# P.V of each two-head unit as one block of matmuls in a windowed attention ahead of two FFNs

## The chip, the cores and the metric

One core of one Trainium2 chip. The metric is device microseconds of one launch, the median of three runs. The kernel has four stages on the same core, one after the other: attention, the first FFN, the second FFN, and the stores. Engines are named as the profile names them: PE is TensorE (its matmuls), PEld its weight loads, DVE is VectorE, ACT is ScalarE, POOL is GpSimd, SP issues most DMAs. L270 is line 270 of the kernel before.

## The reference

`q`, `k`, `v` are (4, 8, 576, 64) in float32: 4 batches, 8 heads, 576 positions, head size 64.

```python
scores = scale * np.matmul(q, k.transpose(0, 1, 3, 2))
bias = slopes[:, None, None] * (-np.abs(rel).astype(np.float32))[None, :, :]
mask = (rel >= 0) & (rel < window)          # window = 128
scores = np.where(mask, scores + bias[None], -1000000000.0)
attn = np.exp(scores - np.max(scores, axis=-1, keepdims=True))
attn = attn / (np.sum(attn, axis=-1, keepdims=True) + 1e-09)
x = np.matmul(attn, v)                      # then laid out as (2304, 512)
h = x @ w_in;  g = h * (1.0 / (1.0 + np.exp(-1.702 * h)));  x = g @ w_out
h = x @ w_in;  g = np.where(h >= 1, h, np.where(h <= -1, 0, (h + 1) ** 2 / 4));  x = g @ w_out
```

Each FFN is 512 to 2048 to 512; its weights arrive as 64-bit floats.

## The kernel before, in words

Attention is cut into 16 **units**, one batch and one pair of heads each. A unit has five **steps**, m = 0 to 4, of 128 queries (the last of 64). For a step, two groups of 64 queries of both heads are multiplied with the 192 keys that the window lets them see. The work of a unit is:

- `load_qk`, `load_v`: the DMAs (L162 to L180).
- `trans_qk` (L192): q and k are transposed on PE in three pieces, copied out of PSUM by DVE and ACT (L195, L198). The third piece has only 64 rows.
- `scores` (L209): the score matmuls of a step into one of three `ps_s` banks; DVE adds the bias and takes the maximum (L217) into one of five `p` buffers, ACT takes the exponential (L220).
- `norm`: DVE makes the reciprocal of the sum (L227, L228), POOL multiplies the probabilities with it (L231).
- `trans_p`: PE transposes the probabilities of a step into one of two `ps_t` banks (L246, L247; L253, L254 in the last step), ACT copies them to the tile `pt` (L249 to L256).
- `pv_mm` (L258 to L281): P.V. The matmuls of one portion read key block m - 1 of `v` as weights, 64 columns for each head, and 256 columns of `pt` (128 in the last portion). The heads write partitions 0 to 63 and 64 to 127 of one PSUM bank, `ps_x`. The last portion adds the 64 positions beyond 512 in a second bank `x1`, taken from the pool `ps_a` (L278, L280), and ACT and DVE copy the result to `xt` (L275, L281).

The order in which these functions are called is set by keys: step s = 5u + m calls `scores` at s, `norm` at s + 0.74, `trans_p` at s + 3.5 and, before the change, `pv_mm` at s + 8.05, so a unit's four portions come at four places between the scores and transposes of the next two units. On top of that a scheduler orders each engine's instructions anew; what it made of the keys is seen only in the built order. Every engine then executes its own list in that order.

Meanwhile the weights of the first FFN come in: 32 halves of 512 KB, each converted by five DVE instructions (L59 to L66), one of ACT (L68) and one of POOL (L69). About 15 are converted during attention and the others during the first block of FFN 1. `split_block` (L95, L96) prepares the first block's input from `xt`. FFN 1 runs five blocks of tokens, FFN 2 six; each is a row of matmuls L330 and L381 or L383.

A matmul on float32 is two instructions in the trace: the 128 program matmuls of L270 are 256 there.

Of the kernel before, what the change touches and what calls it, by code (L numbers as in the profile page):

```python
# [10 lines left out]
F32 = mybir.dt.float32  # L11
# [10 lines left out]
P = 128  # L22
# [3 lines left out]
def tile_window_attention_two_ffn(ctx: ExitStack, tc: tile.TileContext, q, k, v, w1_in, w1_out, w2_in, w2_out, out):  # L26
    nc = tc.nc
# [69 lines left out]
            parts.append(xs)  # L97
        return parts

# [1 line left out]
    with ExitStack() as actx:  # L101
        def pool(name, bufs, **kw):
            return actx.enter_context(tc.tile_pool(name=name, bufs=bufs, **kw))
# [7 lines left out]
        ps_a = pool("ps_a", 2, space=PSUM)  # L111
        ps_s = pool("ps_s", 3, space=PSUM)
        ps_t = pool("ps_t", 2, space=PSUM)
        ps_x = pool("ps_x", 1, space=PSUM)
# [36 lines left out]
        NM = 5  # L151
# [103 lines left out]
                nc.scalar.copy(pt[:, n - 2, :], ps[:, 0, :])  # L255
                nc.scalar.copy(pt[0:64, n - 1, :], ps[0:64, 1, :])  # L256

        def pv_mm(u, m):  # L258
            b, hp = units[u]
            d = st[u]  # L260
            pt, vr = d["pt"], d["v"]
            kb = m - 1
            t0 = b * S
            heads = [slice(64 * j, 64 * j + 64) for j in range(2)]
            if m == 1:
                d["x"] = ps_x.tile([P, 512], F32, tag="x", name="ps_x")
            x = d["x"]
            n = 4 if m < NM - 1 else 2
            for r in heads:
                nc.tensor.matmul(  # L270
                    x[r, 128 * kb:128 * kb + 64 * n].rearrange("p (a b) -> p a b", b=64), vr[:, kb, r],
                    pt[:, 4 * kb:4 * kb + n, r], start=(kb == 0), stop=(m == NM - 1), skip_group_check=True)
            if m < NM - 1:
                return
            nc.scalar.copy(xt[hp][:, t0:t0 + 512], x)  # L275
            x1 = ps_a.tile([P, 2, 256], F32, tag="a", name="ps_x1")
            for r in heads:
                nc.tensor.matmul(x1[r, 0, 0:64], vr[:, kb, r], pt[:, 4 * kb + 2, r], start=True, stop=False)  # L278
            for r in heads:
                nc.tensor.matmul(x1[r, 0, 0:64], vr[0:64, m, r], pt[0:64, 4 * kb + 3, r], start=False, stop=True)  # L280
            nc.vector.tensor_copy(xt[hp][:, t0 + 512:t0 + S], x1[:, 0, 0:64])  # L281

        ev = []
# [1 line left out]
        def at(key, fn, *args):  # L285
            ev.append((key, len(ev), fn, args))
# [4 lines left out]
        for u in range(NU):  # L291
            if u > 0:
                at(5 * u - 2.87, load_qk, u)
                at(5 * u - 13.98, load_v, u)
            for c in range(3):
                at(5 * u - 1.58 + c * 1.49 if u > 0 else -99 + c, trans_qk, u, c)
            for m in range(NM):
                s = 5 * u + m
                at(s, scores, u, m)
                at(s + 0.74, norm, u, m)  # L300
                at(s + 3.5, trans_p, u, m)
                if m > 0:
                    at(s + 8.05, pv_mm, u, m)
        for f in range(SPLIT):
            for i in range(2):
                at(19.59 + 9.45 * (f + 0.5 * i), load_w1, f, i)
# [1 line left out]
            fn(*args)  # L308
        xs0 = split_block(0, B1[0])

# [1 line left out]
    w_b = ctx.enter_context(tc.tile_pool(name="w_b", bufs=NF - SPLIT, reuse_waits="tile"))  # L312
    g_p = ctx.enter_context(tc.tile_pool(name="g_p", bufs=2, reuse_waits="tile"))
    ps_o = ctx.enter_context(tc.tile_pool(name="ps_o", bufs=5, space=PSUM, reuse_waits="tile"))
# [148 lines left out]
```

## Time and profile before

| what | us |
|---|---|
| median of 3 runs (lowest, highest) | 996.01 (995.71, 996.92) |
| span of the profiled execution, first to last instruction | 995.0 |
| median less that span | 1.0 |
| PE busy, share of the span | 967.3, 97% |
| DVE busy | 581.0, 58% |
| ACT busy | 382.9, 38% |
| POOL busy | 160.8, 16% |

The page gives no time of the profiled execution but its span. The span has two unlike parts. Up to about 162 us it is attention, with PE, DVE and ACT all busy most of the time; after that it is the FFNs, in which PE is busy nearly always, and DVE beside it only while weights are converted (to about 248 us, and again at about 500 to 650 us). The busy shares of the whole span hide this, so the views by stage and the chain of work are what to read.

### The profile page before, as it was taken

The numbers are of one execution on the slowest core, as the hardware profiler recorded it, in microseconds if no ns is written. First come the engines' busy times: TensorE is split into PE (matmuls) and PEld (weight loads), VectorE is DVE, ScalarE is ACT, GpSimd is POOL, SyncE is SP. The second block draws the span as 40 slices with busy tenths as digits, with TensorE's granted clock in tenths as the row PEclk, the third lists the DMA queues.
The fourth block names the chain that finished last, engine by engine and source line by source line (L and its number), as shares of the span: only waits on it lengthen the run. The fifth ranks groups of instructions, "written<-read, shape, count | busy, mean of one in ns | idle before, by whom it ended". The sixth has DMA issues, their size and how long they took to land.

```text
span 995.0 us, 13850 instructions
## 1 busy us (share of the span) xinstructions
PE 967.3 (97%) x5024; PEld 837.6 (84%) x5024; DVE 581.0 (58%) x1403; ACT 382.9 (38%) x928; POOL 160.8 (16%) x232
## 2 busy tenths in 40 slices
PE   7999999997999999999999899999999999999998
PEld 5767777876889999999888789789999999999997
DVE  5788889999422422422379999953444444434443
ACT  5898886323222322322333333342332322423322
POOL 4565564232000000000023223300000000000000
PEclk9999999999999999999999999999999999999999
DMA  5565543333000000000013323200000000000000
GB/s 135 150 150 149 147 130 106 119 127 127 1 1 1 1 0 1 1 1 1 1 45 127 126 85 121 91 32 1 1 32 1 13 20 1 33 1 1 32 1 33
DMA packets 81972, 53.33 MB, mean 54 GB/s; under 512 B 58992, under 2 KB 75632, under 8 KB 81904
## 3 DMA queue, kind: packets, MB, share of 16 engines
q1 hardware_dynamic: 81760, 52.31, 18.0%
q8 instruction: 40, 0.66, 0.3%
q14 instruction: 28, 0.23, 0.1%
q10 hardware_dynamic: 144, 0.13, 0.0%
HBM read 47.71 MB, written 4.72 MB: 53 GB/s over the span
## 4 chain that ended last, share of the span: by engine, by line
PE 84%; DVE 11%; issue 2%; SPq 1%; ACT 1%; DMA 0%; POOL 0%; DVEq 0%; POOLq 0%
PE ph L330 35%; PE o L383 17%; PE o L381 17%; PE ps_s L209 4%; PE ps_x L270 4%; DVE x L62 2%; PE ps_qk L192 2%; DVE x L64 2%; PE ps_t L246 2%; DVE x L60 1%; PE ps_t L247 1%; DVE x L66 1%; DVE gs L343 1%; DVE x L59 1%; DVE xs L96 1%
## 5 line engine op out<-in xcount | busy, mean ns | idle before, releaser
L330 PE MATMUL ph<-xs,w 128*128 128x384 f32 (+2 forms) x2112 | 434.1, 354 | 3.4 <-ACT xs L95 1.9
L330 PEld LDWEIGHTS ph<-xs,w 128*128 128x128 f32 x2112 | 386.6, 189 | 34.3 <-DVE xs L96 2.7
L381 PE MATMUL o<-gs,w 128*128 128x460 f32 (+1 forms) x960 | 216.2, 374 | 10.2 <-ACT gs L342 9.2
L383 PE MATMUL o<-w,gs 128*128 128x512 f32 x864 | 216.8, 395 | 2.4 <-ACT gs L342 2.3
L381 PEld LDWEIGHTS o<-gs,w 128*128 128x128 f32 x960 | 180.4, 189 | 34.4 <-ACT gs L342 12.7
L383 PEld LDWEIGHTS o<-w,gs 128*128 128x128 f32 x864 | 160.8, 188 | 34.3 <-ACT gs L342 3.8
L342 ACT CAST gs<-ph 128x384 fp32r<-128x384 f32 (+2 forms) x176 | 89.5, 508 | 188.0 <-DVE ph L341 115.9
L69 POOL TENSOR_TENSOR w<-x,w 128x512 fp32r<-128x512 f32 x64 | 86.2, 1348 | 422.8 <-ACT w L68 419.4
L343 DVE TENSOR_TENSOR gs<-ph,gs 128x384 fp32r<-128x384 f32 (+2 forms) x176 | 104.3, 592 | 77.7 <-ACT gs L342 77.5
L340 DVE TENSOR_TENSOR ph<-ph,ga 128x384 f32<-128x384 f32 x96 | 54.2, 564 | 142.7 <-ACT ga L339 142.7
L337 DVE TENSOR_TENSOR ph<-ph,ga 128x460 f32<-128x460 f32 (+1 forms) x80 | 51.4, 642 | 142.2 <-ACT ga L336 142.2
L339 ACT ACTIVATE ga<-ph,half 128x384 f32<-128x384 f32 x96 | 55.8, 581 | 140.7 <-PE ph L330 135.4
L336 ACT ACTIVATE ga<-ph 128x460 f32<-128x460 f32 (+1 forms) x80 | 44.3, 554 | 152.6 <-PE ph L330 152.4
L231 POOL TENSOR_SCALAR p<-p,sm 128x192 f32<-128x192 f32 (+1 forms) x144 | 69.9, 497 | 64.7 <-DVE sm L228 25.7
L68 ACT CAST w<-x 128x512 fp32r<-128x512 f32 x64 | 39.6, 621 | 85.5 <-DVE x L66 84.2
L220 ACT ACTIVATE p<-p,sm 128x192 f32<-128x192 f32 (+1 forms) x144 | 62.0, 433 | 11.1 <-DVE sm L217 9.8
L209 PE MATMUL ps_s<-kt,q 128*128 128x192 f32 (+2 forms) x288 | 60.1, 329 | 0.0
L341 DVE SCALAR_TENSOR_TENSOR ph<-ga,ph 128x384 f32<-128x384 f32 x96 | 53.8, 560 | 2.8
L217 DVE CUSTOM_DVE_ANT_0 p<-ps_s,bias 128x192 f32<-128x192 f32 (+1 forms) x144 | 45.2, 329 | 15.8 <-PE ps_s L209 12.6
L62 DVE TENSOR_SCALAR x<-x 128x512 int32<-128x512 int32 x64 | 49.6, 776 | 1.2
L209 PEld LDWEIGHTS ps_s<-kt,q 128*128 128x128 f32 x288 | 44.7, 196 | 6.1 <-ACT pt L251 1.5
L64 DVE SCALAR_TENSOR_TENSOR x<-raw,x 128x512 int32<-128x512 int32 x64 | 45.9, 719 | 1.3
(57 smaller groups left out, 601.0 us busy)
## 6 DMA issues: line engine op xcount, KB each, us to landing
raw<-in_moe_w_in_dram SPq DMA_DIRECT2D x32, 512.0 KB, 3.7
raw<-in_moe_w_out_dram SPq DMA_DIRECT2D x32, 512.0 KB, 3.5
out_dram<-ob SPq DMA_DIRECT2D x17, 256.0 KB, 2.0
vraw<-in_v_dram SPq DMA_DIRECT2D x32, 128.0 KB, 2.6
qkraw<-in_q_dram SPq DMA_DIRECT2D x30, 128.0 KB, 2.7
qkraw<-in_k_dram SPq DMA_DIRECT2D x30, 128.0 KB, 2.6
qkraw<-in_q_dram SPq DMA_DIRECT2D x16, 32.0 KB, 2.4
qkraw<-in_k_dram SPq DMA_DIRECT2D x16, 32.0 KB, 2.4
```

The source lines that it names most:

```text
L62: nc.vector.tensor_scalar(out=x, in0=x, scalar1=3, scalar2=0x3FFFFFF8, op0=ALU.logical_shift_left, op1=ALU.bitwise_and)
L64: nc.vector.scalar_tensor_tensor(out=x, in0=lo, scalar=29, in1=x, op0=ALU.logical_shift_right, op1=ALU.bitwise_or)
L69: nc.gpsimd.tensor_tensor(out=w[:, 1, i, :], in0=f32(x), in1=f32(w[:, 0, i, :]), op=ALU.subtract)
L209: nc.tensor.matmul(ps[:, e, lo:192], d["q"][:, i, :], d["k"][:, 64 * i - 128 + lo:64 * i + 64], start=True, stop=True)
L220: nc.scalar.activation(x, x, AF.Exp, bias=sm[:, 0, e:e + 1], scale=-1.0, accum_out=sm[:, 1, e:e + 1])
L231: nc.gpsimd.tensor_scalar(out=x, in0=x, scalar1=sm[:, 2, e:e + 1], scalar2=1.0, op0=ALU.mult, op1=ALU.mult)
L330: nc.tensor.matmul(ph, w[f][:, a, 0, c * P:(c + 1) * P], xs[j][c][:, b, :], start=(c == 0 and i == 0), stop=(c == KC - 1 and i == 2))
L339: nc.scalar.activation(a, ph, AF.Relu, scale=0.5, bias=half)
L342: nc.scalar.copy(gs[:, 0, :], ph)
L343: act_last[0] = nc.vector.tensor_tensor(out=gs[:, 1, :], in0=ph, in1=f32(gs[:, 0, :]), op=ALU.subtract)
L381: nc.tensor.matmul(o[j][m][:, 0:n], w[f][:, a, 1, sl], gs[:, b, :], start=first, stop=last)
L383: nc.tensor.matmul(o[j][m], gs[:, b, sl], w[f][:, a, 1, :], start=first, stop=last)
```

## The change

`pv_mm(u, m)`, called four times for a unit, becomes `pv_unit(u)`, called once at the key of the former last portion. It issues the same matmuls on the same operands, those of the bank `x` first and then those of `x1`, and then the two copies. The key of every other function is as before.

```diff
-        def pv_mm(u, m):
+        def pv_unit(u):
...
-            kb = m - 1
...
-            if m == 1:
-                d["x"] = ps_x.tile([P, 512], F32, tag="x", name="ps_x")
-            x = d["x"]
-            n = 4 if m < NM - 1 else 2
+            x = ps_x.tile([P, 512], F32, tag="x", name="ps_x")
+            x1 = ps_a.tile([P, 2, 256], F32, tag="a", name="ps_x1")
+            last = NM - 1
+            for kb in range(last):
+                n = 4 if kb < last - 1 else 2
+                for r in heads:
+                    nc.tensor.matmul(
+                        x[r, 128 * kb:128 * kb + 64 * n].rearrange("p (a b) -> p a b", b=64), vr[:, kb, r],
+                        pt[:, 4 * kb:4 * kb + n, r], start=(kb == 0), stop=(kb == last - 1), skip_group_check=True)
             for r in heads:
-                nc.tensor.matmul(
-                    x[r, 128 * kb:128 * kb + 64 * n].rearrange("p (a b) -> p a b", b=64), vr[:, kb, r],
-                    pt[:, 4 * kb:4 * kb + n, r], start=(kb == 0), stop=(m == NM - 1), skip_group_check=True)
-            if m < NM - 1:
-                return
+                nc.tensor.matmul(x1[r, 0, 0:64], vr[:, last - 1, r], pt[:, 4 * last - 2, r], start=True, stop=False)
+            for r in heads:
+                nc.tensor.matmul(x1[r, 0, 0:64], vr[0:64, last, r], pt[0:64, 4 * last - 1, r], start=False, stop=True)
             nc.scalar.copy(xt[hp][:, t0:t0 + 512], x)
...
-                if m > 0:
-                    at(s + 8.05, pv_mm, u, m)
+            at(5 * u + 4 + 8.05, pv_unit, u)
```

The scheduler makes its own order of this, so a unit's matmuls are not one uninterrupted run on PE. In the built order L274 and L276 are the former L278 and L280, and the line numbers from there on are lower by 4. A **cluster** below is a run of P.V matmuls with nothing else of PE between them. In the order before there are 66 clusters; in the order of the change there are 39.

PE around the second step of a unit, before (`p_107` and `p_108` are the probability buffers of steps 1 and 2, `q_112` the queries of the next unit; the second pair of transposes of a step is left out):

```order
L270 MATMUL ps_x<-pt,vraw 64x256 x2
L246 MATMUL ps_t<-ident,p_107 128x128
L247 MATMUL ps_t<-ident,p_107 128x128
...
L192 MATMUL ps_qk<-ident,qkraw 128x128 x4
L270 MATMUL ps_x<-pt,vraw 64x256
L209 MATMUL ps_s<-kt,q_112 128x64
L209 MATMUL ps_s<-kt,q_112 128x128
L270 MATMUL ps_x<-pt,vraw 64x256
L246 MATMUL ps_t<-ident,p_108 128x128
```

The same place in the changed order:

```order
L192 MATMUL ps_qk<-ident,qkraw 128x128
L246 MATMUL ps_t<-ident,p_107 128x128
L247 MATMUL ps_t<-ident,p_107 128x128
...
L192 MATMUL ps_qk<-ident,qkraw 128x128 x3
L270 MATMUL ps_x<-pt,vraw 64x256 x3
L209 MATMUL ps_s<-kt,q_112 128x64
L209 MATMUL ps_s<-kt,q_112 128x128
L246 MATMUL ps_t<-ident,p_108 128x128
```

Three clusters of two, one and one matmuls have become one of three, ahead of the next unit's first scores.

PE further on in the same unit, before (steps 3 and 4):

```order
L209 MATMUL ps_s<-kt,q_112 128x192 x2
L270 MATMUL ps_x<-pt,vraw 64x256 x2
L192 MATMUL ps_qk<-ident,qkraw 128x64 x2
L246 MATMUL ps_t<-ident,p_109 128x128
...
L209 MATMUL ps_s<-kt,q_112 128x192 x2
L270 MATMUL ps_x<-pt,vraw 64x128 x2
L278 MATMUL ps_x_605<-pt,vraw 64x64 x2
L280 MATMUL ps_x_605<-pt,vraw 64x64 x2
L253 MATMUL ps_t<-ident,p_110 128x128
```

The same place in the changed order:

```order
L209 MATMUL ps_s<-kt,q_112 128x192 x2
L192 MATMUL ps_qk<-ident,qkraw 128x64 x2
L246 MATMUL ps_t<-ident,p_109 128x128
...
L209 MATMUL ps_s<-kt,q_112 128x192 x2
L270 MATMUL ps_x<-pt,vraw 64x256 x3
L270 MATMUL ps_x<-pt,vraw 64x128 x2
L274 MATMUL ps_x_596<-pt,vraw 64x64 x2
L276 MATMUL ps_x_596<-pt,vraw 64x64 x2
L253 MATMUL ps_t<-ident,p_110 128x128
```

The cluster ahead of the 64-row transposes L192 is gone, and its matmuls stand in the unit's last cluster.

POOL around step 3, the same in the two orders at this place (`p_108` and `p_109` belong to steps 2 and 3):

```order
L231 TENSOR_SCALAR p_108<-p_108,sm 128x192 x2
L69 TENSOR_TENSOR w<-x,w 128x512
L231 TENSOR_SCALAR p_109<-p_109,sm 128x192 x2
```

A weight's instruction L69 stands directly ahead of the two normalisations of step 3 in 4 units of the order before and in 5 of the changed one.

## Rows read from the trace of the kernel before

**Rows 1.** Busy time by stage: stretch, its length, each engine (instructions), PE clock.

```profile
core 0: us, PE busy (x) PEld busy (x) DVE busy (x) ACT busy (x) POOL busy (x), PEclk, DMA share, GB/s
20.00:162.00 142.00, 141.10 (x1030) 101.71 (x1029) 119.81 (x588) 126.30 (x436) 84.25 (x149) 1.00 0.56 142
162.00:210.00 48.00, 46.93 (x223) 41.50 (x222) 46.71 (x74) 16.67 (x30) 14.48 (x11) 1.00 0.36 116
210.00:250.00 40.00, 32.37 (x143) 26.52 (x142) 37.90 (x61) 13.14 (x25) 9.15 (x7) 0.98 0.38 124
```

**Rows 2.** The chain that ended last, 60 to 66 us: start, length, engine, tile, line.

```profile
60.03 0.58 PE ps_x L270 x4
60.62 0.26 PE ps_t L246
60.88 0.11 PE ps_t L247
60.99 0.11 PE ps_t L246
...
61.64 0.57 PE ps_x L270 x2
62.22 0.64 PE ps_s L209 x4
62.86 0.58 PE ps_x L270 x2
63.44 0.26 PE ps_t L246
...
64.68 0.58 PE ps_x L270 x4
65.26 0.27 PE ps_qk L192 x2
65.53 0.26 PE ps_t L246
```

**Rows 3.** The same chain at two longer clusters.

```profile
99.30 1.01 PE ps_x L270 x6
...
152.85 1.66 PE ps_x L270 x14
```

**Rows 4.** Groups by line, 0 to 225 us: P.V matmuls and their weight loads.

```profile
L270 PE MATMUL ps_x<-pt,vraw 128*64 128x256 f32 (+1 forms) x256 | 45.3, 374 | 0.0
L270 PEld LDWEIGHTS ps_x<-pt,vraw 128*64 128x64 f32 x256 | 16.8, 135 | 15.0 <-issue 11.4 <-ACT pt L256 0.9
```

**Rows 5.** The same chain where the 64-row transposes follow scores, not P.V.

```profile
148.39 0.65 PE ps_s L209 x4
149.05 0.27 PE ps_qk L192 x2
149.31 0.26 PE ps_t L246
```

**Rows 6.** The same chain where the weights' conversion carries it, in FFN 1's first block.

```profile
226.32 1.50 DVE x L62
227.84 0.70 DVE x L64
228.57 0.70 DVE x L66
229.29 0.62 ACT w L68
229.91 0.49 ACT gs L342
```

**Rows 7.** Timeline of PE: step 3's scores in two units, its transposes in the first.

```profile
58.24 0.33 PE L209 MATMUL ps_s<-kt,q 128*128 128x192 f32 x1
...
65.46 0.33 PE L246 MATMUL ps_t<-ident,p 128*128 128x128 f32 x1
...
77.20 0.49 PE L209 MATMUL ps_s<-kt,q 128*128 128x192 f32 x2
```

**Rows 8.** Timeline of POOL in the second of these units.

```profile
81.72 1.27 POOL L69 TENSOR_TENSOR w<-x,w 128x512 fp32r<-128x512 f32 x1
82.97 0.59 POOL L231 TENSOR_SCALAR p<-p,sm 128x192 f32<-128x192 f32 x1
```

More of the change, by code (lines that the diff above doesn't have):

```diff
@@ L261, in pv_mm @@
             pt, vr = d["pt"], d["v"]
-            kb = m - 1
             t0 = b * S
             heads = [slice(64 * j, 64 * j + 64) for j in range(2)]
-            if m == 1:
-                d["x"] = ps_x.tile([P, 512], F32, tag="x", name="ps_x")
-            x = d["x"]
-            n = 4 if m < NM - 1 else 2
-            for r in heads:
-                nc.tensor.matmul(
-                    x[r, 128 * kb:128 * kb + 64 * n].rearrange("p (a b) -> p a b", b=64), vr[:, kb, r],
-                    pt[:, 4 * kb:4 * kb + n, r], start=(kb == 0), stop=(m == NM - 1), skip_group_check=True)
-            if m < NM - 1:
-                return
-            nc.scalar.copy(xt[hp][:, t0:t0 + 512], x)
[L276 to L280, printed above, removed]
+            x = ps_x.tile([P, 512], F32, tag="x", name="ps_x")
[7 more added lines that the diff above has]
+                        pt[:, 4 * kb:4 * kb + n, r], start=(kb == 0), stop=(kb == last - 1), skip_group_check=True)
+            for r in heads:
+                nc.tensor.matmul(x1[r, 0, 0:64], vr[:, last - 1, r], pt[:, 4 * last - 2, r], start=True, stop=False)
+            for r in heads:
+                nc.tensor.matmul(x1[r, 0, 0:64], vr[0:64, last, r], pt[0:64, 4 * last - 1, r], start=False, stop=True)
+            nc.scalar.copy(xt[hp][:, t0:t0 + 512], x)
             nc.vector.tensor_copy(xt[hp][:, t0 + 512:t0 + S], x1[:, 0, 0:64])
```

## The prediction

> **What bounds the kernel now.** I began with the busy time by stage [rows 1], since shares of the whole span mix two kernels. From 20 to 162 us, nearly all of attention, PE is busy for 141.1 of 142 us, but ACT is busy for 126.3 (89%) and DVE for 119.8 (84%), so that view alone doesn't settle which of them sets the pace. The chain of work does: from 60 to 66 us [rows 2] every piece is a PE instruction released by the PE instruction before it, and so it goes on through the attention stage. What shortens PE's own list there should shorten the stage, as long as the other engines keep up.
>
> The reader should see three things in those rows. A cluster of one pair of matmuls, one for each head (x4 in the trace), lasts 0.58 us. A cluster with a single matmul (x2) lasts 0.57 us, just as long: the two heads run beside each other, and a lone one leaves its partner's place empty. And the first transpose behind a cluster takes 0.26 us where the following ones take 0.11, so each cluster also makes its follower 0.15 us longer.
>
> From 162 us the limit is another. DVE is busy for 46.7 of 48 us and then 37.9 of 40 [rows 1], and late in this stretch the chain goes through the conversion of weights [rows 6]. That work is fixed and waits for nothing of the change. In both orders 15 of the 32 halves are converted ahead of the last unit's copy on DVE, so the rest begins earlier by what attention ends earlier, and the gain should arrive at the end undiminished.
>
> **What the change removes.** The matmuls themselves stay. What goes is the cost of starting and ending a cluster. Its price comes from longer clusters [rows 3]: x6 is two pair slots and takes 1.01 us, so a further slot costs 1.01 - 0.58 = 0.43 us. The long one confirms it: three full slots and one of half width are 0.58 + 0.43 + 0.43 + 0.22 = 1.66. A one-slot cluster costs 0.58 + 0.15 = 0.73 us, of which 0.43 is work; **0.30 us is the price of having a cluster**. The weight loads tell of the same thing: they sat idle for 15.0 us ahead of L270, 11.4 of it with no releaser ("issue") [rows 4], which is 0.23 us for each of 66 clusters.
>
> Would merging also fill empty places? No: counted by slots of 256 columns, a lone matmul counting as a full slot, the order before needs 63 and the changed one 63 too, since the scheduler again cuts runs at odd places. So only the fixed price counts: 66 - 39 = 27 clusters by 0.30 us are 8.1 us.
>
> One correction. Ten of the removed clusters stood directly ahead of the 64-row transposes L192. There the followers are 0.27 and 0.26 us [rows 2], and where the same transposes follow scores they are 0.27 and 0.26 as well [rows 5]. The delay behind the cluster belongs to those transposes and stays. These ten save 0.58 - 0.43 = 0.15 us each instead of 0.30, which takes 1.5 us off. **PE's list becomes 6.6 us shorter.**
>
> **What it adds.** The distance from scores to the transposes of the same step shrinks, and the chain DVE, ACT, DVE, POOL has to fit into it. The tightest is step 3. Before, its scores began at 58.24 and its transposes at 65.46 [rows 7], 7.22 us later, with four clusters in between: the four of [rows 2], whose shares are 0.73, 0.57, 0.73 and 0.58 (the second and the fourth without a follower's delay that goes). In the changed order one of two slots (1.01) stands there instead, and the distance is 7.22 - 2.61 + 1.01 = 5.6 us. POOL's worst case is step 3 with a weight's L69 ahead of it: scores at 77.20 [rows 7], L69 for 1.27 us, the last normalisation done at 82.97 + 0.59 = 83.56 [rows 8], which is 6.4 us after the scores. Where no L69 is in the way, POOL is done sooner by about that 1.27 us, 5.1, and fits. L69 stands there in 5 units of the changed order; those with more slots between have some 0.4 us more distance. So a few tenths may be lost in some units: from nothing to 5 times 0.8 = 4.0 us. I take 0.6, near the lower end, because before the change PE's chain shows no POOL in these rows and the L69 that costs most is one unit's worst case.
>
> Edits costed at nothing: the two copies at a unit's end stay one each and still follow the last matmul; `x1` is taken earlier in the program but written at the same place in PE's list; `pt` and `v` are last read by the same portion as before, so no DMA starts later; SP's list only swaps one weight load with a `v` load. ACT covers the shorter stage: 126.3 us of work in 142 - 6.6 = 135.4 is 93%, DVE 88%. If that cover were gone, the loss would be the second rival below.
>
> **Sum.** -6.6 + 0.6 = -6.0 us. The profiled span of 995.0 becomes 989.0; the median of the runs lies 1.0 us above the span, so 996.0 becomes **990.0 us**. A measurement can tell about 0.2% (2.0 us) from no change; this is three times that.
>
> **Rivals.**
>
> *The waits give back more.* Step 3's distance is short in every unit, not only behind L69. At the upper bound of 4.0 us the time is 996.0 - 6.6 + 4.0 = 993.4. For it: three engines at 84 to 99% leave little room for bunched scores. Against: in the changed order the scores of step 3 stand behind the unit's last cluster, so POOL has that long to finish steps 0 to 2 first, and it is busy for only 84.3 of 142 us [rows 1].
>
> *ACT is the real bound.* Occupancy of ACT is 89%, and PE's busy time counts overlapping ends that are modelled. If ACT's list sets the pace, PE just waits where it worked, and the time stays at 996.0. For it: the weight loads fill only 101.7 of 142 us, 72% [rows 1]. Against: the chain holds no ACT piece in [rows 2], and ACT has 142 - 126.3 = 15.7 us idle to give, over twice what is asked of it. The Trainium skill, Perfetto Trace Analysis, section Identifying the Most-Contended Engine, calls the engine with the highest occupancy the most contended, and wants TensorE judged by its weight loads and not by its matmuls. By that rule ACT would come first here and the saving on PE would be worth nothing: this rival. The chain speaks against the rule in this stage, since the holes in the weight loads are themselves PE's price for a cluster.
>
> *PE ends up waiting for POOL, and it gets slower.* The mechanism is L69 on POOL between the statistics and the normalisations of step 3. Done 6.4 us after the scores against a distance of 5.6, it stalls PE by 0.8 us; in all 16 units that is 12.8, and the time 996.0 - 6.6 + 12.8 = 1002.2. It decides from 6.6 / 16 = 0.41 us in each unit on. Against it: L69 stands there in 5 units and not in 16, and a stall gives POOL time to catch up.
>
> *More than the sum.* The change doesn't quite do what it says, since 39 clusters remain where 16 would be one for a unit; but if the correction for L192 is wrong, all 8.1 us arrive with no new wait: 987.9.
>
> **How the numbers follow.** The forecast, 989.0 to 992.0, has 0.60; the larger give-back, 992.0 to 994.6, 0.20, of which 0.03 lies within 0.2%; the larger gain, 987.8 to 989.0, 0.07; ACT as the bound, 0.07; POOL's stall, 0.06. Faster by over 0.2% is 0.60 + 0.17 + 0.07 = 0.84, within 0.2% is 0.03 + 0.07 = 0.10, slower 0.06. The range 987.8 to 994.0 leaves out ACT's and POOL's cases and the 0.03, 0.16 in all.
>
> **What would show it.** Right: weight loads' idle time ahead of P.V falls from 15.0 us to about 39 times 0.23 = 9; clusters of up to ten trace matmuls at 0.43 us a slot; the first FFN matmul some 6 us earlier and everything behind it shifted by the same. Wrong: POOL or ACT pieces in the chain inside attention (the waits), gaps on PE ahead of L246 in step 3 (POOL's stall), an unchanged end of attention with ACT near 95% (ACT's bound), or a DVE stretch behind attention that still ends at about 248 us, which would mean that the conversion had not moved along.

## The result, and the profile after

The changed kernel takes **985.8 us** (985.5 to 986.2) against 996.2 for the kernel before in the same session: 10.4 us less, a ratio of 0.9899 [0.9885, 0.9913]. The forecast was 990.0 and its range began at 987.8, so the sign was right and the size was not.

The page of the changed kernel, its span and busy times:

```profile
span 984.3 us, 13841 instructions
PE 958.9 (97%) x5024; PEld 841.7 (86%) x5024; DVE 578.1 (59%) x1403; ACT 381.1 (39%) x928; POOL 162.1 (16%) x232
```

Busy time by stage in the changed kernel, columns as in [rows 1], the stages shifted by the 6 us by which the first FFN row came earlier (the third is cut 2 us shorter, so that it holds about as many instructions as before):

```profile
20.00:156.00 136.00, 135.01 (x1037) 106.14 (x1038) 121.44 (x596) 125.52 (x438) 86.67 (x151) 1.00 0.59 150
156.00:204.00 48.00, 46.92 (x223) 41.77 (x222) 45.84 (x75) 16.43 (x29) 13.32 (x11) 1.00 0.37 117
204.00:242.00 38.00, 32.48 (x149) 27.27 (x148) 35.89 (x59) 12.83 (x26) 9.21 (x7) 1.00 0.38 125
```

Attention is shorter with about the same work on ACT and DVE; ACT is now busy for 92% of it, and PE still nearly all the time. The second stretch is as it was. The third does the work of 40 us in 38.

To see where the 10.7 us of span went, I follow four marks through both traces: the first score of unit 1, the last score, and FFN **rows** (the L330 matmuls of one f; row 0 is the first of FFN 1's first block, row 16 opens the second block).

| stretch | before | after | difference |
|---|---|---|---|
| start to unit 1's first score | 17.07 | 18.00 | +0.9 |
| unit 1's first score to last score | 135.46 | 128.19 | **-7.3** |
| last score to row 3 | 20.50 | 20.77 | +0.3 |
| row 3 to row 10 | 35.38 | 35.38 | 0.0 |
| row 10 to row 17 | 46.49 | 42.31 | **-4.2** |
| row 17 to row 64 | 235.39 | 235.40 | 0.0 |
| row 64 to row 96 (weights of FFN 2) | 160.65 | 160.15 | -0.5 |
| row 96 to row 175 | 331.9 | 331.9 | 0.0 |

Two thirds of the gain are attention's. A third appears 50 us behind attention, in code that the change doesn't touch.

**Attention.** The chain of waits in the changed kernel (start, length, what), at the place of [rows 2]:

```profile
59.43 0.22 PE ps_qk L192 x2
59.65 1.01 PE ps_x L270 x6
60.65 0.64 PE ps_s L209 x4
61.30 0.11 PE ps_t L246
...
61.73 0.65 PE ps_s L209 x4
62.38 0.26 PE ps_qk L192 x2
...
63.89 0.85 PE ps_x L270 x7
64.74 0.06 PE ps_x L274
```

The two-slot cluster takes the 1.01 us that it was priced at, scores pass straight to transposes at 0.11 us, and from 20 to 140 us no engine but PE is in the chain. PE is busy without a gap there (columns as above):

```profile
20.00:140.00 120.00, 120.00 (x922) 95.99 (x924) 107.00 (x545) 112.20 (x398) 75.18 (x136) 1.00 0.62 155
```

**Behind attention.** Two things differ. The first is DVE's conversion. (A 33rd and 34th conversion, the first two of FFN 2's weights, follow the 32 of FFN 1 directly.) Before, of the 20 L60 and 20 L62 between the 14th and the 34th conversion, 15 take about 1.45 us instead of 0.43, each of them beside an L69 on POOL. One of them in the timelines of DVE and POOL before (start, length, engine, line):

```profile
207.99 0.43 DVE L60 TENSOR_SCALAR x<-x 128x512 f32<-128x512 f32 x1
208.45 1.48 DVE L62 TENSOR_SCALAR x<-x 128x512 int32<-128x512 int32 x1
```

```profile
208.35 1.29 POOL L69 TENSOR_TENSOR w<-x,w 128x512 fp32r<-128x512 f32 x1 [3.35 <-ACT w L68]
```

L62 begins 0.10 us after L69 and ends 0.29 us after it ends. I call this a **collision**. [rows 6] hold one too: 1.50 us for L62. In the changed kernel 11 L60 and L62, one L64 and one L66 collide. From L66 of the 14th conversion to the end of L66 of the 34th DVE takes 89.2 us before and 86.4 after. DVE's order differs (16 conversions are finished ahead of FFN 1's first L337 before, 17 after), but from row 10 on about as many conversions stand ahead of each row's L337 in both (28 and 29 at row 10, 33 and 33 at row 13). Groups by line, row 3 to row 17, before and then after (count, then busy time, mean ns, idle time ahead):

```profile
L330 PE MATMUL ph<-xs,w 128*128 128x462 f32 (+1 forms) x169 | 39.8, 384 | 2.0 <-ACT xs L95 1.7 <-DVE xs L96 0.3
L381 PE MATMUL o<-gs,w 128*128 128x462 f32 x169 | 38.5, 376 | 5.6 <-ACT gs L342 5.6
L62 DVE TENSOR_SCALAR x<-x 128x512 int32<-128x512 int32 x17 | 15.7, 926 | 0.5
L60 DVE TENSOR_SCALAR x<-x 128x512 f32<-128x512 f32 x17 | 13.7, 806 | 0.4
```

```profile
L377 PE MATMUL o<-gs,w 128*128 128x462 f32 x169 | 38.3, 374 | 4.3 <-ACT gs L338 4.3
L326 PE MATMUL ph<-xs,w 128*128 128x462 f32 (+1 forms) x168 | 38.0, 374 | 1.2 <-ACT xs L95 0.9 <-DVE xs L96 0.3
L62 DVE TENSOR_SCALAR x<-x 128x512 int32<-128x512 int32 x17 | 14.7, 863 | 0.4
L60 DVE TENSOR_SCALAR x<-x 128x512 f32<-128x512 f32 x16 | 11.1, 696 | 0.3
```

PE idles for 7.6 us before and for 5.5 after, 5.6 and 4.3 of it ahead of L381 (L377 after), for activations whose DVE instructions stand in one queue with the conversion.

The second is PE's clock. Where the conversion ends, before and then after (columns as in [rows 1]):

```profile
246.00:248.00 2.00, 0.27 (x1) 0.19 (x1) 1.39 (x4) 1.34 (x3) 0.00 (x0) 1.00 0.40 135
248.00:250.00 2.00, 1.74 (x5) 1.37 (x5) 2.00 (x5) 1.56 (x4) 0.00 (x0) 0.60 0.32 127
250.00:252.00 2.00, 2.00 (x7) 1.71 (x7) 1.26 (x3) 0.54 (x1) 0.00 (x0) 0.54 0.00 0
```

```profile
238.00:240.00 2.00, 0.80 (x3) 0.43 (x3) 1.48 (x3) 2.00 (x5) 0.00 (x0) 1.00 0.75 254
240.00:242.00 2.00, 2.00 (x11) 1.79 (x11) 1.90 (x4) 0.91 (x3) 0.00 (x0) 1.00 0.02 8
```

Before, PE has hardly worked for 2 us, and the granted clock then is at the lower of its two levels for 3.4 us; row 16 to row 17 takes 7.17 us. After, PE's hole is shorter, the clock stays at 1.00, and the same distance is 5.63: 1.5 of the 4.2 us. The other 2.6 come between row 10 and row 16, about the 2.8 us by which DVE's conversions are shorter. Two collisions fewer, of some 1.0 us each, are 2.1 of these; I did not trace the rest.

### The profile page after: what moved, and what is told of

Same layout as the page of the kernel before. It is cut to its first block, busy times and chain, and to the rows that moved or that the text cites. A ratio compares the mean times of both kernels' runs of the same rounds, so it can differ in the third digit from the quotient of the medians.

```text
span 984.3 us, 13841 instructions
## 1 busy us (share of the span) xinstructions
PE 958.9 (97%) x5024; PEld 841.7 (86%) x5024; DVE 578.1 (59%) x1403; ACT 381.1 (39%) x928; POOL 162.1 (16%) x232
## 4 chain that ended last, share of the span: by engine, by line
PE 83%; DVE 11%; issue 3%; SPq 1%; DMA 1%; ACT 1%; POOL 0%; DVEq 0%; POOLq 0%
PE ph L326 35%; PE o L379 19%; PE o L377 15%; PE ps_s L209 4%; PE ps_x L270 3%; DVE x L62 2%; DVE x L64 2%; PE ps_qk L192 2%; DVE x L60 2%; DVE x L66 1%; PE ps_t L246 1%; PE ps_t L247 1%; DVE gs L339 1%; DVE x L59 1%; DVE xs L96 1%
## 5 line engine op out<-in xcount | busy, mean ns | idle before, releaser
L377 PE MATMUL o<-gs,w 128*128 128x460 f32 (+1 forms) x960 | 216.4, 374 | 10.0 <-ACT gs L338 9.0
L377 PEld LDWEIGHTS o<-gs,w 128*128 128x128 f32 x960 | 181.0, 189 | 33.9 <-ACT gs L338 12.3
L69 POOL TENSOR_TENSOR w<-x,w 128x512 fp32r<-128x512 f32 x64 | 87.3, 1367 | 415.9 <-ACT w L68 411.0
L209 PE MATMUL ps_s<-kt,q 128*128 128x192 f32 (+2 forms) x288 | 59.8, 331 | 0.0
L337 DVE SCALAR_TENSOR_TENSOR ph<-ga,ph 128x384 f32<-128x384 f32 x96 | 53.8, 561 | 2.8
L62 DVE TENSOR_SCALAR x<-x 128x512 int32<-128x512 int32 x64 | 50.7, 793 | 1.1
L209 PEld LDWEIGHTS ps_s<-kt,q 128*128 128x128 f32 x288 | 45.1, 199 | 5.5 <-ACT pt L251 2.3
L64 DVE SCALAR_TENSOR_TENSOR x<-raw,x 128x512 int32<-128x512 int32 x64 | 46.6, 730 | 0.9
```

What stands on the lines that cost most here:

```text
L62: nc.vector.tensor_scalar(out=x, in0=x, scalar1=3, scalar2=0x3FFFFFF8, op0=ALU.logical_shift_left, op1=ALU.bitwise_and)
L64: nc.vector.scalar_tensor_tensor(out=x, in0=lo, scalar=29, in1=x, op0=ALU.logical_shift_right, op1=ALU.bitwise_or)
L69: nc.gpsimd.tensor_tensor(out=w[:, 1, i, :], in0=f32(x), in1=f32(w[:, 0, i, :]), op=ALU.subtract)
L209: nc.tensor.matmul(ps[:, e, lo:192], d["q"][:, i, :], d["k"][:, 64 * i - 128 + lo:64 * i + 64], start=True, stop=True)
L377: nc.tensor.matmul(o[j][m][:, 0:n], w[f][:, a, 1, sl], gs[:, b, :], start=first, stop=last)
```

## The experiments

The theory after the result: the price of a cluster and of nothing else shortened attention, and the 4.2 us behind it are a change in the collisions between DVE's conversion and POOL's L69, since the scheduler gave DVE another order. The rival: the 4.2 us belong to the change itself, as conversion that moved along or matmuls that run otherwise. All kernels compute the whole result. "Attention" below is from unit 1's first score to the last score, "conversion" from row 3 to row 17, both in the profiled execution. Each ratio is to the kernel before in the same session; its median was 996.2 us with the changed kernel, 996.6 with the first four kernels below it and 997.8 with the last four, so medians of different sessions compare to about 1.5 us.

| kernel | median us (lowest, highest) | ratio [interval] | attention | conversion |
|---|---|---|---|---|
| before | 996.2 (995.7, 996.9) | 1 | 135.46 | 81.87 |
| after | 985.8 (985.5, 986.2) | 0.9899 [0.9885, 0.9913] | 128.19 | 77.69 |
| before_low_on_dve | 985.5 (984.7, 986.3) | 0.9888 [0.9873, 0.9903] | 135.46 | 70.68 |
| after_low_on_dve | 977.7 (976.9, 978.5) | 0.981 [0.9795, 0.9825] | 128.26 | 70.69 |
| one_run_per_unit | 987.4 (986.3, 988.3) | 0.9909 [0.989, 0.9928] | 129.48 | 76.11 |
| one_run_low_on_dve | 981.7 (981.5, 982.4) | 0.9852 [0.9837, 0.9866] | 129.75 | 70.68 |
| two_parts_low_on_dve | 979.2 (978.9, 979.7) | 0.982 [0.9805, 0.9835] | 130.22 | 70.69 |
| four_pinned_low_on_dve | 978.6 (977.9, 979.5) | 0.9814 [0.9799, 0.9829] | 130.45 | 70.68 |
| one_run_qk_early | 977.7 (977.2, 978.3) | 0.9805 [0.979, 0.982] | 121.06 | 70.68 |
| all_low_on_dve | 968.8 (968.1, 969.2) | 0.9715 [0.9699, 0.9731] | 128.25 | 70.69 |

### Both kernels without L69 on POOL behind attention

The subtraction L69 of the last 19 halves of FFN 1's weights goes to DVE, in the kernel before and in the changed one.

```diff
-        nc.gpsimd.tensor_tensor(out=w[:, 1, i, :], in0=f32(x), in1=f32(w[:, 0, i, :]), op=ALU.subtract)
+        (sub or nc.gpsimd).tensor_tensor(out=w[:, 1, i, :], in0=f32(x), in1=f32(w[:, 0, i, :]), op=ALU.subtract)
...
-            load_half(src, w, i)
+            load_half(src, w, i, nc.vector if w_in is w1_in and 2 * f + i >= 13 else None)
```

> The kernel before, with the subtraction L69 of weight halves 13 to 31 moved from POOL to DVE. Theory A (the extra 4 us of the change come from fewer collisions: behind attention, L60 and L62 on DVE run 1.0 us longer whenever L69 runs on POOL, 15 times before and 11 times after): no long L60 or L62 is left there, DVE's work falls by 15 x 1.03 and rises by 19 x 0.55 us, net -5.0 us; time 990 to 992, gap between the two kernels with this edit near the attention part alone, 6 to 7 us. Theory B (collisions don't matter, the change simply let the conversions start and run sooner): long ones vanish or not, time rises by up to 10 us for the added DVE work, or stays, and the gap stays at 10.4 us.

> The changed kernel with the same edit. Theory A: 13 collisions of 1.03 us go, 19 x 0.55 us come, net -2.9 us; time 983 to 984.5, so 6 to 7 us under the kernel before with this edit. Theory B: 985.8 or slower, and 10.4 us under the kernel before with this edit.

Groups by line from row 3 to row 17 in before_low_on_dve; the two lines of PE and three of DVE:

```profile
L330 PE MATMUL ph<-xs,w 128*128 128x462 f32 (+1 forms) x169 | 38.0, 372 | 0.0
L381 PE MATMUL o<-gs,w 128*128 128x462 f32 x168 | 37.6, 372 | 0.0
...
L69 DVE TENSOR_TENSOR w<-x,w 128x512 fp32r<-128x512 f32 x15 | 10.3, 685 | 0.0
...
L62 DVE TENSOR_SCALAR x<-x 128x512 int32<-128x512 int32 x17 | 7.2, 421 | 0.1
...
L60 DVE TENSOR_SCALAR x<-x 128x512 f32<-128x512 f32 x16 | 6.8, 423 | 0.2
```

No L60 or L62 is long any more, PE waits for nothing, and the chain from row 3 to row 17 is PE alone, and the conversion stretch takes 70.68 us in the one kernel and 70.69 in the other: **the 4.2 us are gone once L69 is off POOL**, and what remains between the two kernels is 7.8 us in the medians, about attention's 7.2 (128.26 - 135.46). That settles the main question: the extra gain went by way of the conversion with L69 on POOL and is no part of what the change does to P.V.

The expected sizes were too small (5.0 us for the kernel before, 2.9 for the changed one; measured 11.2 and 7.0 in the stretch). They counted DVE's saved time. But from the 14th to the 34th conversion the kernel before still takes 86.7 us instead of 89.2, only 2.5 less; what vanishes is PE's waiting (7.6 us above) and the half clock. That fits PE waiting for the short FFN instructions that stand behind a collision in DVE's queue. But the edit also let the scheduler order DVE anew: ahead of row 13's L337 33 conversions stand before and 30 here. How the 11.2 us divide between the collisions and this order is not shown.

### One uninterrupted run for each unit

Here PE's order is pinned, so that the 16 units have 16 clusters and 48 slots, with L69 on POOL as before and with L69 on DVE.

```diff
         for key, _, fn, args in sorted(ev, key=lambda e: e[:2]):
-            fn(*args)
+            with ExitStack() as order:
+                for name, last in (pe_last if fn is pv_unit else {"pv": pe_last.get("pv")}).items():
+                    if last is not None and fn in (scores, trans_p, trans_qk, pv_unit):
+                        order.enter_context(tc.issue_after(last.ins))
+                fn(*args)
```

(This is the core of the edit. `pe_last` holds the last matmul of each kind so far, and `issue_after` keeps what is called next behind it.)

> The changed kernel with PE's order pinned so that each unit's P.V is one cluster: 16 clusters instead of 39, and 48 full slots instead of 63. Theory C (a cluster costs 0.30 us and a slot 0.43): PE's list in attention is 23 x 0.30 + 15 x 0.43 = 13.4 us shorter; since ACT is at 93% it can give no more than about 8 of it; time 976 to 981, with ACT or POOL waits in the chain inside attention. Rival D (a block of 2 us on PE starves DVE, ACT and POOL, and the waits behind it eat the gain): attention no shorter than in the changed kernel, time 985 or more.

> Both edits on the changed kernel: 16 clusters, and L69 of halves 13 to 31 on DVE. If the two act in different stages, their gains add: one_run_per_unit less 2 to 3 us (theory A with C). If the conversions' pace only shifts with attention (B), it is no faster than one_run_per_unit.

Attention takes 129.48 us, 1.3 more than with the scheduler's 39 clusters: here it is the waits that decide. Busy time and the waits of one_run_per_unit from 20 to 140 us (engine, tile, line, what it waited for: us in total, times, longest), and its chain:

```profile
20.00:140.00 120.00, 111.81 (x914) 92.66 (x914) 111.61 (x546) 112.82 (x398) 72.27 (x134) 1.00 0.62 156
```

```profile
PE ps_s L209 <- ACT q L198: 7.0, 12, 1.4
```

```profile
72.44 1.69 PE ps_x L270 x16
...
76.22 0.64 ACT p L220 x3
76.85 0.17 issue
77.02 0.19 ACT p L220
77.20 0.26 ACT q L198
77.46 0.01 issue
77.47 0.38 ACT q L198
77.85 0.04 issue
77.89 0.71 PE ps_s L209 x4
```

The run itself costs less than the clusters it replaces, but the next unit's first scores follow soon behind it and wait for the copies of their own q, which stand behind exponentials and other copies on ACT. PE is busy for only 111.8 of 120 us. The conversion stretch tells something else: 12 long instructions on DVE between row 3 and row 17, as many as after (before has 13), and yet 76.11 us, less than after's 77.69. L66 of its 14th conversion began 9.5 us ahead of row 0, in the other two 4.5. So the number of collisions alone doesn't give the time; the head start of the conversions counts too. With L69 on DVE 5.7 us come off the median, where 2 to 3 were expected.

### Between: two parts, and four parts pinned

Two calls for each unit instead of one (44 clusters, 62 slots), unpinned; and the four portions of the kernel before, pinned as above, so that both heads always run together (61 clusters, 48 slots). Both with L69 on DVE. The core of the first:

```diff
-        def pv_unit(u):
+        def pv_unit(u, half):
...
-            for kb in range(last):
+            for kb in range(2 * half, 2 * half + 2):
...
-            at(5 * u + 4 + 8.05, pv_unit, u)
+            for half in range(2):
+                at(5 * u + 2 + 2 * half + 8.05, pv_unit, u, half)
```

> The changed kernel with P.V called in two parts for a unit instead of one, and L69 of halves 13 to 31 on DVE, so that collisions behind attention play no part: 44 clusters, 62 slots, none ahead of the 64-row transposes. If the attention part of the gain is the number of clusters (0.30 us each, 0.15 for those ahead of the 64-row transposes), it stands between the two kernels with that edit (66 clusters 985.5, 39 clusters 977.7): attention 5.5 to 6.0 us shorter than with 66 clusters, time 979 to 980.5. If the gain hangs on something else than the count (the place of the single run, say), the time lies at either end, 977.7 or 985.5.

> The kernel before with its four portions, PE's order pinned so that no portion is cut in two, and L69 of halves 13 to 31 on DVE: 61 clusters but 48 full slots instead of 63. If a lone matmul costs a whole slot, 15 slots by 0.43 and 2.1 us for the clusters come off PE's list, 8.5 us: time about 977 without new waits, and 981 if waits as in one_run_per_unit take half. If a lone matmul costs nothing extra, about 2 us come off: 983.5.

Two parts: 22 clusters fewer than before, attention 5.2 us shorter, 0.24 us for each; the change has 27 fewer and 7.3, 0.27 for each. So attention follows the number of clusters. Four pinned: 5 clusters fewer, but 15 slots, because no matmul runs alone; attention is 5.0 us shorter. By the prices of the prediction that should have been 15 x 0.43 + 5 x 0.30 = 8.0. So lone matmuls do cost, but 3 us of that price didn't arrive. Added up from the start of each PE instruction to the start of the next, P.V lost 6.8 us, nearly the 15 x 0.43 + 5 x 0.15 = 7.2 of its share; what stands around it took 1.7 us more, where 5 x 0.15 = 0.8 less was due. About half of that 1.7 is gaps on PE (it is busy for 119.06 us from 20 to 140).

### One run, with q and k transposed earlier

If the wait for ACT's copies is what one run costs, q and k should be transposed sooner.

```diff
-                at(5 * u - 2.87, load_qk, u)
+                at(5 * u - 4.6, load_qk, u)
...
-                at(5 * u - 1.58 + c * 1.49 if u > 0 else -99 + c, trans_qk, u, c)
+                at(5 * u - 3.2 + c * 1.49 if u > 0 else -99 + c, trans_qk, u, c)
```

> one_run_low_on_dve with the transposes of the next unit's q and k, and their loads, called 1.6 steps earlier. In one_run_per_unit the scores wait for ACT's copy of q (7.0 us in 12 waits) because those transposes stand behind the run of P.V. If that is what ate the gain of the single run, the waits go and the time falls from 981.7 to 973 to 977. If ACT and DVE at 93 to 94% are the limit by now, it stays at 980 to 982.

Attention falls from 129.75 to 121.06 us, PE is busy for 119.28 us from 20 to 140, and the wait of L209 for q is gone: it was the cost. The time falls only from 981.7 to 977.7, just short of the 973 to 977 expected. Unit 1's first score comes later (20.10 us), and the last unit pays. Busy time at the end of attention in this kernel:

```profile
144.00:146.00 2.00, 0.00 (x0) 0.00 (x0) 1.97 (x6) 0.71 (x2) 0.47 (x1) 0.71 0.47 164
146.00:148.00 2.00, 1.29 (x4) 0.58 (x4) 1.64 (x4) 0.87 (x2) 1.99 (x3) 0.50 0.50 152
148.00:150.00 2.00, 2.00 (x11) 1.23 (x12) 1.30 (x3) 1.54 (x3) 0.38 (x1) 0.50 0.32 119
```

PE does nothing for 2 us. In the chain this is DVE with a weight's L62, L64 and L66, then POOL with the last probabilities; L64 takes 1.63 us, beside an L69 that POOL had begun 0.34 us before it. The granted clock falls to the lower level; the last run of P.V takes 3.19 us in the chain where a run takes 1.69 at 72.44 us above. From last score to row 0 is 13.0 us, against 9.3 in the changed kernel.

### L69 off POOL in FFN 2 as well

```diff
-            load_half(src, w, i, nc.vector if w_in is w1_in and 2 * f + i >= 13 else None)
+            load_half(src, w, i, nc.vector if w_in is w2_in or 2 * f + i >= 13 else None)
```

> after_low_on_dve with L69 of the second FFN's 32 halves on DVE as well. There too L60 and L62 collide with L69 (16 and 2 long ones at 500 to 640 us). If collisions cost PE time there as they do behind attention, 2 to 5 us more: 973 to 975.5. If PE doesn't wait for the weights there, no change: 977.7.

Groups by line, row 64 to row 96, in after_low_on_dve (L69 still on POOL there) and then in all_low_on_dve:

```profile
L377 PE MATMUL o<-gs,w 128*128 128x462 f32 (+1 forms) x217 | 50.8, 383 | 5.3 <-ACT gs L338 3.2 <-DVE gs L339 2.1
...
L62 DVE TENSOR_SCALAR x<-x 128x512 int32<-128x512 int32 x30 | 26.9, 900 | 0.5
```

```profile
L377 PE MATMUL o<-gs,w 128*128 128x462 f32 (+1 forms) x217 | 48.4, 372 | 0.0
...
L62 DVE TENSOR_SCALAR x<-x 128x512 int32<-128x512 int32 x30 | 12.4, 420 | 0.1
```

The same mechanism at a second place: L62 returns to 0.42 us, PE's wait ahead of L377 is gone, and the half-clock stretch of 3.4 us that after_low_on_dve has at 562 us is gone with it. The stretch falls from 160.20 to 151.27 us, by 8.9 where 2 to 5 were expected. At **968.8 us** this kernel beats both, the changed one by about 17 us.

### The two kernels profiled again

> The kernel before, unchanged, in a second profiled execution. If the number of long L60 and L62 behind attention is set by the order of DVE and POOL, it stays at 15 (give or take 1) and the distance from the FFN row with index 3 to the one with index 17 stays at 81.9 us, give or take 1; the half-clock stretch at about 248 us comes again. If the number is a matter of chance in each execution, it moves by 3 or more and the distance by 3 us or more, and then the 4.2 us by which this distance fell in the changed kernel are not the change's.

> The changed kernel, unchanged, in a second profiled execution. By the order: 11 long L60 and L62 (give or take 1), the distance between the same two FFN rows 77.7 us, give or take 1, no half-clock stretch near 240 us. By chance: the number moves by 3 or more. From the first score of unit 1 to the last score 128.2 us, give or take 0.3, by both.

Neither kernel is edited. Before: 15 long instructions again, conversion 81.85 us (81.87), attention 135.45 (135.46), the half clock again at the conversion's end. After: 11 and the two others again, 77.72 (77.69) and 128.23 (128.19), no half clock there. So the collisions are set by the order and repeat. What doesn't repeat is the start: unit 1's first score came at 17.07 and 17.88 us before, at 18.00 and 17.11 after. From that mark to the end of the span it is 978.0 and 977.7 before, 966.3 both times after: 11.5 us.

## Why the prediction was wrong

**What failed: "That work is fixed and waits for nothing of the change ... and the gain should arrive at the end undiminished."** The gain did arrive undiminished as far as row 10 (-6.1 us there, the later start included) and was then increased. The work of converting is fixed, but its duration on DVE is not: it depends on which instructions meet L69 on POOL, and that on DVE's order, which the scheduler made anew. Taking L69 off POOL removed the 4.2 us in this stretch; from unit 1's first score to the end the two kernels then differ by 7.1 us instead of 11.5. The sign of this was luck: I know of nothing in the change that favours fewer collisions. The row that should have stopped me is in [rows 6], which I used only to say that the chain passes there: L62 at 1.50 us, beside 0.43 for the same instruction elsewhere.

The Trainium skill, SBUF — State Buffer, section SBUF: two separate sides, says that GpSimd shares one pair of ports with VectorE, which needs it in its two-port modes or, against a GpSimd instruction that reads SBUF, with two inputs in SBUF; whoever starts first holds it for its whole instruction and the other is blocked. The trace agrees: at 208.45, 212.83 and 221.60 us before, L60 or L62 ended 0.28 to 0.29 us after the L69 that had begun ahead of it. The page alone would not have told how many collisions the new order has.

**PE's list, -6.6 us forecast.** The price of a cluster was right, if low: attention is 7.3 us shorter for 27 fewer clusters. Added up from start to start, P.V lost 4.2 us (forecast 27 x 0.15 = 4.05) and what stands around it 3.0 (forecast 17 x 0.15 = 2.55): 1.9 at the scores, 0.7 at L246, 0.6 at the L192 of 128 rows and nothing at those of 64. What was mis-sized is the correction for the ten clusters ahead of the 64-row L192. The prediction set a cluster's second 0.15 us wholly behind it. By the starts before the change, 0.09 of it lies ahead (a 192-column L209 is followed after 0.256 us if a cluster comes next, else after 0.163) and 0.06 behind (an L246 is followed after 0.168 instead of 0.109). So the 64-row transposes (3.97 us in both kernels) kept only the smaller part, and ten times 0.09 us that the forecast had taken off came too, about what it lacked.

**The allowance for waits, +0.6 us.** It was not needed: PE has no gap from 20 to 140 us, and neither POOL nor ACT stands in the chain there. Step 3's distance did shrink to the 5.6 us worked out (5.61 in four units), but POOL was done 4.48 us after the scores in these; where it took 5.7 to 6.5, the distance was 6.0 to 6.8, but for the last unit. Together these two terms were 1.3 us off. With them alone the time would have been in the range.

**The weight loads' idle time ahead of P.V**, forecast at 9 us from 15.0 [rows 4], is 12.6:

```profile
L270 PEld LDWEIGHTS ps_x<-pt,vraw 128*64 128x64 f32 x256 | 18.9, 136 | 12.6 <-issue 6.3 <-ACT xt L277 0.8 <-ACT pt L256 0.2
```

Its part without a releaser fell from 11.4 to 6.3, in proportion to the clusters (11.4 x 39 / 66 = 6.7). The forecast had scaled the whole of it.

**The rivals.** ACT as the bound fell: its work went from 89% to 92% of a shorter stage. The Trainium skill, Perfetto Trace Analysis, section Identifying the Most-Contended Engine, would have put ACT first; the 7.3 us that came off PE's list speak against that rule in this stage. POOL's stall at step 3 did not come. Yet the idea behind both, that merged matmuls bunch the scores and leave another engine late, is right one step further on: with 16 clusters instead of 39, PE waits 7.0 us for ACT's copies of q. The scheduler's odd cuts, which I counted as a failure of the change to do what it says, are what kept that wait away.

## What to carry to other kernels

Price the switches between kinds of matmul from the chain, by comparing a short run with a longer one, and take with it the delay of the instructions on both sides; but don't merge to the end, since what stands behind a long run must have been prepared before it. When an edit lets a scheduler reorder an engine, no stretch of that engine's work is fixed: look in it for one instruction with two durations, and find what lies beside the long ones. Where a busy engine's short instructions stand behind such collisions, try one of the two partners on another engine: here that gave 11.2 us of a stretch in which it took 2.5 us off DVE, with a share of the new order that isn't separated.

## What the hardware showed that I had not expected

- A DVE instruction of 0.43 us (L60, L62) took 1.33 to 1.55 us behind attention if it began within 0.3 us after POOL's L69, and ended 0.28 to 0.29 us after it; one that began 0.99 us after it (187.28 us before) took 0.60. L64 and L66, 0.69 us alone, took 1.77 and 1.67 (169.92 and 161.51 us after). The same subtraction takes 0.685 us on DVE and 1.3 to 1.4 on POOL, so here even the busier engine is the better place for it.
- A hole in PE's work can be paid for twice: the granted clock fell to 0.5 at 248.4 us before, just behind a hole of 1.7 us, and stayed there for 3.4 us; in one_run_qk_early it fell at 144.8 us, 0.9 us into a hole of 2.6 us, and stayed for 6.8 us. But holes of 1.9 and 2.1 us at 547 and 560 us of that same run left it at 1.00.
- The start varies by 0.9 us between executions of one kernel, with a half-clock stretch in one of two executions of the changed kernel (at 15.1 us) and none in the other.
